# Global-filter mixing and a SoLU layer on one core: the opening's x from one queue, tables and weights requested during the first step

## The chip, the cores and the metric

The kernel runs on one core of one Trainium2 chip. The metric is the device time of one execution in microseconds (us). A core has TensorE (PE; its weight loads are listed as PEld), VectorE (DVE), ScalarE (ACT), GpSimd (POOL) and SyncE (SP). SP, ACT and POOL each have a queue on which they request DMA transfers; SP's and ACT's queues are of the hardware kind (q1 and q10 in the profile), POOL's is of the software kind (q0).

## The reference, cut to what matters

```python
# x: (8, 3136, 256); filt_r, filt_i: (1569, 256); float32
X = np.fft.rfft(x, axis=1)                       # along the sequence
Y = X * (filt_r + 1j * filt_i)[None]
x = np.fft.irfft(Y, n=3136, axis=1).reshape(25088, 256)

h = x @ w_in                                     # (25088, 1024), float64 weights in memory
e = np.exp(h - h.max(-1, keepdims=True))
solu = h * e / (e.sum(-1, keepdims=True) + 1e-9)
mu = solu.mean(-1, keepdims=True); var = ((solu - mu) ** 2).mean(-1, keepdims=True)
out = ((solu - mu) / np.sqrt(var + 1e-6) * g_ln) @ w_out   # (25088, 256)
```

## The kernel before

The transform of length 3136 = 49 x 64 is done in steps by matrix products: a first step over 49 rows (with tables `wf`), a second step over the 64 columns (tables `de`), the product with the filter, and the two steps back. Between the steps the data change their layout by going through DRAM (`d1`, `d2`). The first of the eight batch entries is transformed alone, in an opening; the other seven are transformed beside the token blocks of the SoLU layer, step by step, in the long body. The opening also fetches the filter (`f`) and the tables, and fetches and converts the weights from float64.

The opening, cut to what the change and the text below touch. Line numbers in the profile: L465 is the transfer in `fetch_x`, L217 and L219 the product and the copy in `first`, L172 and L173 the two transfers of `by_16`, L425 and L428 the transfers of `load_tables`, L369 those of the weights, L381 to L405 the conversion of a weight, L516 the small fetches of the second step's first unit (t<-x), L282 those of its other units (y<-d), L292 the products of the second step, L492 the idle products, L313 to L315 the product with the filter, L548 the stores to `f_dram`.

```python
def by_16(dmas, out, in_):                       # 100 rows: 96 on one queue, 4 on the other
    n = 45 if out.shape[0] == N1 else out.shape[0] // 16 * 16
    dmas[0](out=out[:n], in_=in_[:n])
    dmas[1](out=out[n:], in_=in_[n:])

# in class Spectrum
def first(self, i, halves, ps, evac, out=None):
    ...
    for j, u in enumerate(halves):
        nc.tensor.matmul(out=ps[0:NK, j], lhsT=wf_t, rhs=self.xs[i][0:NR, 2*u:2*u+2, :], ...)
    evac(out=t1..., in_=ps...)                   # ACT copies back over x

# the opening
def load_tables(i0, n, dma):                     # n of 13 units, from i0
    de = fpool.tile([P, n, 2, 2, NQ], FP32, ...)
    dma(out=de, in_=de_dram[i0:i0 + n]...)
    f = fpool.tile([P, n, 2, C], FP32, ...)
    for place, k, held, rows in all_filter_rows(i0, n):      # 8 transfers
        dma(out=f[place, 0:held, k, :], in_=rows)

def begin(j): raws[j] = load_words(weights[j][1], j)         # POOL requests a weight, 512 KB

rows_x = pools["r"].tile([P, NH, C], FP32, name="x_0", tag="r")
def fetch_x(h, n0, n, r0, rows, dma):            # h = 0: columns upwards; h = 1: downwards
    first, step = (n0, C) if h == 0 else (N2 - 1 - n0, -C)
    dma(out=rows_x[N1*h + r0:N1*h + r0 + rows, n0:n0 + n], in_=...)

nc.sync.dma_start(out=wf_t, in_=wf_dram)
pieces = NH // NCH                               # 8 pieces of 4 columns
fetch_x(0, 0, NCH, 0, N1 - 1, nc.sync.dma_start)
fetch_x(0, 0, NH, N1 - 1, 1, nc.sync.dma_start)
for i in range(pieces):
    if i:
        fetch_x(0, NCH * i, NCH, 0, N1 - 1, nc.sync.dma_start)
    fetch_x(1, NCH * i, NCH, 0, N1, nc.gpsimd.dma_start)
    if i in (4, 7):
        begin(i // 7)                            # weights 0 and 1
load_tables(0, 4, nc.gpsimd.dma_start)
load_tables(4, 4, nc.gpsimd.dma_start)
for i in range(pieces):                          # the first step
    sp.xs[i] = rows_x[:, NCH * i:NCH * i + NCH]
    sp.first(i, (0, 1), ..., nc.scalar.copy, sp.xs[i][0:NK])
    sp.store_first(i, 0, lambda out, in_: by_16((nc.scalar.dma_start, nc.sync.dma_start), out, in_))

idle_row(8, "idle")                              # products of tables[0] that keep TensorE busy
for j in range(2):
    convert(j)                                   # VectorE, ACT (L400) and POOL: weights 0 and 1

sp.t2s[0] = t2_0 = pools["t2"].tile([P, 4, C], FP32, ...)
for n in range(16):                              # t<-x, 32 KB each, in turns on SP and ACT
    (nc.sync, nc.scalar)[n % 2].dma_start(out=t2_0[NH*(n%4):NH*(n%4)+NH, n//4, :],
                                          in_=rows_x[n:n + 1])
for i in range(1, units):                        # y<-d, 512 KB each (the last 128 KB)
    sp.fetch(i, nc.sync.dma_start, spare_piece(i - 1))
    if i == 2:
        load_tables(8, NP - 8, nc.sync.dma_start)
for i in range(2):
    start(i)                                     # pb: forward product of unit i
for i in range(units):                           # 7 units
    if i + 2 < units:
        start(i + 2)
    sp.multiply(i, 0, nc.vector.tensor_tensor)   # VectorE
    sp.multiply(i, 1, nc.gpsimd.tensor_tensor)   # VectorE and POOL
    ...                                          # inverse product, store; begin(2) to begin(6)
...                                              # step back, weights 2 to 7, fetch of entry 1
for i0, n, rows in ((0, 4, P), (4, 4, P), (8, NP - 9, P), (NP - 1, 1, NQ)):
    f, at = filters[i0]
    nc.sync.dma_start(out=f_dram[i0:i0 + n]..., in_=f[0:rows, at:at + n]...)
```

Of the kernel before, what the change touches and what calls it, by code (L numbers as in the profile page):

```python
# [17 lines left out]
P = 128  # L18
# [5 lines left out]
N1, N2 = 49, 64  # L24
NH = N2 // 2
NS, NQ = (N1 + 1) // 2, 64
NP = (NS + 1) // 2
NR = 2 * N1
NK = 4 * NS
NCH = 4  # L30
# [62 lines left out]
def kernel(  # L93
# [10 lines left out]
    nc = tc.nc  # L104
# [52 lines left out]
    def all_filter_rows(i0, n):  # L157

        for k, filt in enumerate((filt_r, filt_i)):
            for u in range(2):  # L160
                for quarter in range(2):
                    held = min(n, (NS - u + 1) // 2 - i0)
                    yield (slice(NQ * u + 32 * quarter, NQ * u + 32 * quarter + 32), k, held,
                           filter_rows(filt, quarter, u, i0, held))
# [4 lines left out]
    def by_16(dmas, out, in_):  # L169
# [5 lines that stand above are left out]
    class Spectrum:  # L175
# [24 lines left out]
        def fetch_x(self, i, halves, out=None):  # L200
            if out is None:
                out = self.pools["r"].tile([P, NCH, C], FP32, name=f"x_{self.e}_{i}", tag="r")
            self.xs[i] = out
            xb = x[self.e]
            for h, first, step in ((0, NCH * i, C), (1, N2 - 1 - NCH * i, -C)):
                halves[h](out[N1 * h:N1 * h + N1],
                          bass.AP(tensor=xb.tensor, offset=xb.offset + first * C,
                                  ap=[[N2 * C, N1], [step, NCH], [1, C]]))
# [151 lines left out]
    with ExitStack() as st:  # L360
# [6 lines left out]
        def load_words(src, n):  # L367
            raw = wpool.tile([P, 512, 2], I32, name=f"raw_{n}", tag="raw")
            nc.gpsimd.dma_start(  # L369
                out=raw.rearrange("p (k d) w -> p k d w", d=src.shape[-2]) if len(src.shape) == 4 else raw,  # L370
                in_=src)
            return raw
# [45 lines left out]
        def fetch_second():  # L418
            for i in range(6):
                second.fetch_x(i, [lambda out, in_: nc.sync.dma_start(out=out, in_=in_)] * 2,  # L420
                               spare_piece(i))

        def load_tables(i0, n, dma):
            de = fpool.tile([P, n, 2, 2, NQ], FP32, name=f"de_{i0}", tag=f"de{i0}")
            dma(out=de, in_=de_dram[i0:i0 + n].rearrange("i p k u q -> p i (k u q)"))  # L425
            f = fpool.tile([P, n, 2, C], FP32, name=f"f_{i0}", tag=f"f{i0}")
            for place, k, held, rows in all_filter_rows(i0, n):
                dma(out=f[place, 0:held, k, :], in_=rows)  # L428
            for i in range(n):
                tables[i0 + i], filters[i0 + i] = (de, i), (f, i)  # L430
# [12 lines left out]
        def resident(held):  # L443
            def find(sp, u):
                i, pairs = sp.units[u]
                tile, at = held[i]
                return tile[:, at:at + pairs]
            return find

        sp = Spectrum(0, pools, resident(filters), resident(tables))  # L450
        raws = {}

        def begin(j):
            raws[j] = load_words(weights[j][1], j)
# [15 lines left out]
        nc.sync.dma_start(out=wf_t, in_=wf_dram)  # L470
        pieces = NH // NCH

        fetch_x(0, 0, NCH, 0, N1 - 1, nc.sync.dma_start)
        fetch_x(0, 0, NH, N1 - 1, 1, nc.sync.dma_start)
        for i in range(pieces):
            if i:
                fetch_x(0, NCH * i, NCH, 0, N1 - 1, nc.sync.dma_start)
            fetch_x(1, NCH * i, NCH, 0, N1, nc.gpsimd.dma_start)
            if i in (4, 7):
                begin(i // 7)  # L480
        load_tables(0, 4, nc.gpsimd.dma_start)
        load_tables(4, 4, nc.gpsimd.dma_start)
        for i in range(pieces):
            sp.xs[i] = rows_x[:, NCH * i:NCH * i + NCH]

            sp.first(i, (0, 1), ps_h.tile([P, 2, 512], FP32, name=f"pa_0_{i}", tag="h"),
                     nc.scalar.copy, sp.xs[i][0:NK])
            sp.store_first(i, 0, lambda out, in_: by_16((nc.scalar.dma_start, nc.sync.dma_start), out, in_))

        def idle(out):  # L490

# [23 lines left out]
        for n in range(16):  # L515
            (nc.sync, nc.scalar)[n % 2].dma_start(  # L516
                out=t2_0[NH * (n % 4):NH * (n % 4) + NH, n // 4, :], in_=rows_x[n:n + 1])
# [25 lines left out]
        for ch in range(pieces):  # L543
            fetch_back(0, ch, None, by_16)
        fetch_second()
        for i0, n, rows in ((0, 4, P), (4, 4, P), (8, NP - 9, P), (NP - 1, 1, NQ)):
            f, at = filters[i0]
            nc.sync.dma_start(  # L548
                out=f_dram[i0:i0 + n].rearrange("i u q k c -> (u q) i (k c)")[0:rows],
                in_=f[0:rows, at:at + n].rearrange("p i k c -> p i (k c)"))  # L550
# [283 lines left out]
    for e in range(1, B):  # L834
        first_at, spectrum_at, back_at = PLAN[e]
        sp = Spectrum(e, pools, load_filter, load_de)
        if e == 1:
            sp = second
# [178 lines left out]
```

## Time and profile before

| | |
|---|---|
| time, median of 3 runs | 1681.72 us (1679.47 to 1682.98) |
| span of the profiled execution | 1680.2 us |
| PE, PEld, DVE, ACT, POOL busy | 95%, 65%, 75%, 56%, 67% |
| first matmul of the opening starts | 9.34 us |
| last store of the first step requested by ACT | 28.49 us |
| first product of the second step (pb) starts | 45.28 us |
| fourth unit's rows requested, used | 53.51, 59.24 us |
| mean DMA rate, whole span; 0 to 130 us | 186; 264 GB/s |

The profile comes from one execution, taken by the hardware profiler. Engine rows give busy time and what ended the idle time before a group of instructions; a row `t<-x` names the tile written and the tile read. A row with ACTq, SPq or POOL and DMA_DIRECT2D is the request of a transfer, not the transfer itself; the transfer's landing is seen in who was released by it. The chain of waits is followed back from the last instruction to what released it at each step. PEclk is the granted TensorE clock, where 1.00 is full speed.

### The profile page before, as it was taken

The page shows a single profiled execution, that of the slowest core. Times are in us where ns is not written, and L with a number is a line of the kernel's source. Part 1 is how long each engine was busy: PE and PEld are TensorE (multiplying, and loading weights), DVE is VectorE, ACT ScalarE, POOL GpSimd, SP SyncE. Part 2 cuts the span into 40 slices and gives each one's busy share as a digit, 9 for nine tenths or more (in the row PEclk, how much of TensorE's full clock was granted, in tenths as well). Part 3 has the DMA queues.
Part 4 walks back from the last instruction along what each step waited for, and adds up shares of the span by engine and source line. Part 5 has one row for each costly group of instructions (what it writes and reads, how often), then busy time and mean ns, then how long its engine had stood idle before and what let it go on. Part 6 is the DMA issues. An engine that isn't in the chain of part 4 may idle for free.

```text
span 1680.2 us, 31072 instructions
## 1 busy us (share of the span) xinstructions
PE 1597.7 (95%) x10022; PEld 1094.7 (65%) x10022; DVE 1260.4 (75%) x2619; ACT 939.3 (56%) x1730; POOL 1120.8 (67%) x1268
## 2 busy tenths in 40 slices
PE   5798899999999999999999999999999999999996
PEld 1353356766766676667766676667776777777776
DVE  1676887788777877886878777887778767787773
ACT  2154455656655565566655656556565566655551
POOL 4444786577676766697577866687576766676674
PEclk8999999999999999999999999999999999999999
DMA  9886868786787668865786667766775444444443
GB/s 264 254 278 202 255 180 243 196 220 182 191 224 222 178 182 236 228 182 150 210 243 195 176 166 220 229 181 161 204 213 161 117 125 123 103 106 105 109 112 95
DMA packets 375957, 311.72 MB, mean 186 GB/s; under 512 B 61514, under 2 KB 341571, under 8 KB 375795
## 3 DMA queue, kind: packets, MB, share of 16 engines
q1 hardware_dynamic: 306260, 169.81, 38.5%
q0 software_dynamic: 32640, 101.65, 20.5%
q10 hardware_dynamic: 36896, 38.28, 8.2%
q8 instruction: 81, 1.33, 0.3%
q14 instruction: 80, 0.66, 0.1%
HBM read 124.83 MB, written 81.50 MB: 123 GB/s over the span
## 4 chain that ended last, share of the span: by engine, by line
PE 64%; DMA 17%; DVE 8%; POOL 3%; issue 3%; SPq 2%; ACT 1%; ACTq 0%; DVEq 0%; POOLq 0%
PE m L680 26%; PE o L792 25%; DMA solu_t<-turn 7%; PE py L353 5%; DMA x<-in_x_dram 2%; DMA t<-d 2%; PE pa L260 2%; PE pb L292 2%; PE pc L292 2%; SPq L750 2%; DVE h L728 2%; DVE turn L738 1%; DMA out_dram<-ot 1%; PE pa L217 1%; DVE diff L245 1%
## 5 line engine op out<-in xcount | busy, mean ns | idle before, releaser
L730 ACT ACTIVATE e<-h,nmu 128x1024 f32<-128x1024 f32 x196 | 225.3, 1149 | 360.3 <-DVE h L728 358.8
L792 PEld LDWEIGHTS o<-w_out_sb,solu_t 128*128 128x128 f32 x3136 | 380.3, 192 | 57.8 <-issue 40.7
L792 PE MATMUL o<-w_out_sb,solu_t 128*128 128x128 f32 x3136 | 400.5, 276 | 9.1 <-DVE rsum L723 6.3
L680 PE MATMUL m<-w_in_sb,s 128*128 128x512 f32 x784 | 401.8, 604 | 4.6 <-ACT h L690 2.5
L792 PEld LDWEIGHTS o<-w_out_sb,u 128*128 128x128 f32 x2352 | 305.2, 191 | 147.4 <-issue 113.8
L658 POOL TENSOR_TENSOR u<-solu_t 128x512 f32<-128x512 f32 x98 | 145.3, 1483 | 311.0 <-DMA solu_t<-turn 179.0
L680 PE MATMUL m<-w_in_sb,y 128*128 128x512 f32 x588 | 313.8, 617 | 15.9 <-DVE nmax L704 12.8
L792 PE MATMUL o<-w_out_sb,u 128*128 128x128 f32 x2352 | 312.3, 276 | 7.0 <-ACT ot L804 6.3
L728 DVE SCALAR_TENSOR_TENSOR h<-e,rsum,h 128x1024 f32<-128x1024 f32 x196 | 289.1, 1475 | 6.9
L811 DVE SCALAR_TENSOR_TENSOR ot<-o,rs_t,ot 128x128 f32<-128x128 f32 x294 | 102.5, 349 | 206.6 <-ACT ot L804 170.3
L690 ACT COPY h<-m 128x512 f32<-128x512 f32 x294 | 173.5, 590 | 130.8 <-PE m L680 116.2
L738 DVE STREAM_TRANSPOSE turn<-h 128x1024 f32<-128x1024 f32 x196 | 242.3, 1236 | 0.8
L712 ACT ACTIVATE e<-h,nmax 128x1024 f32<-128x1024 f32 x196 | 226.1, 1154 | 0.0
L658 POOL TENSOR_TENSOR u<-solu_t,u 128x512 f32<-128x512 f32 x98 | 142.7, 1456 | 87.2 <-PE o L792 83.3
L704 DVE CUSTOM_DVE_ANT_0 h<-m,h 128x512 f32<-128x512 f32 x196 | 133.2, 679 | 82.2 <-ACT h L690 59.3
L680 PEld LDWEIGHTS m<-w_in_sb,y 128*128 128x128 f32 x588 | 95.1, 192 | 124.5 <-DVE nmax L704 67.9
L356 ACT COPY y<-py 128x392 f32<-128x392 f32 x128 | 109.6, 856 | 105.4 <-PE py L353 103.8
L353 PEld LDWEIGHTS py<-wi_t,t 100*128 100x128 f32 x1024 | 132.3, 192 | 53.9 <-issue 40.4
L680 PEld LDWEIGHTS m<-w_in_sb,s 128*128 128x128 f32 x784 | 124.0, 191 | 65.9 <-issue 45.7
L658 POOL TENSOR_TENSOR solu_t<-solu_t,solu_t 128x512 f32<-128x512 f32 x98 | 150.8, 1538 | 7.7
L658 POOL TENSOR_TENSOR u<-u,solu_t 128x512 f32<-128x512 f32 x98 | 136.9, 1397 | 0.7
L353 PE MATMUL py<-wi_t,t 100*128 100x98 f32 x1024 | 131.6, 273 | 0.7 <-DMA t<-d 0.4
(108 smaller groups left out, 1978.3 us busy)
## 6 DMA issues: line engine op xcount, KB each, us to landing
solu_t<-turn SPq DMA_DIRECT2D x784, 128.0 KB
out_dram<-ot SPq DMA_DIRECT2D x196, 128.0 KB
t<-d POOLq DMA_DIRECT2D x56, 400.0 KB, 4.9
d<-x POOLq DMA_DIRECT2D x100, 200.0 KB, 5.3
f<-f_dram POOLq DMA_DIRECT2D x39, 512.0 KB, 6.9
d<-g POOLq DMA_DIRECT2D x39, 512.0 KB, 5.1
t<-d ACTq DMA_DIRECT2D x36, 512.0 KB
x<-in_x_dram SPq DMA_DIRECT2D x112, 98.0 KB
```

Of the source, the lines that this page charges most:

```text
L353: nc.tensor.matmul(out=psv[:, i:2 * NCH - i:2 * NCH - 1 - 2 * i, :], lhsT=t4s[e, ch][:, i, cb * P:cb * P + P], rhs=wi_t, start=True, stop= ...
L356: evac(out=y[:, cb, t0:t0 + S].rearrange("p (r m j) -> p m j r", m=N2 // NCH, j=NCH)[:, ch:last + 1 - ch:last - 2 * ch], in_=psv.rearrange ...
L658: nc.gpsimd.tensor_tensor(out=out, in0=in0, in1=in1, op=op)
L680: nc.tensor.matmul(out=ms[j, bank], lhsT=lhsT, rhs=w_in_sb[:, w, :], start=m in (1, 2, 7), stop=True, skip_group_check=True)
L690: nc.scalar.copy(out=h_half(k, i), in_=ms[j, 0])
L704: nc.vector.tensor_tensor_reduce(out=h_half(k, i), in0=ms[j, bank], in1=h_half(*kept), scale=1.0, scalar=sofar, op0=ALU.add, op1=ALU.min, ...
L712: nc.scalar.activation(out=e, in_=hs[k], func=AFT.Exp, bias=nmaxs.pop(k)[:, 1:2], scale=-1.0, accum_out=esum)
L728: nc.vector.scalar_tensor_tensor(out=solu, in0=e, scalar=rsum, in1=solu, op0=ALU.mult, op1=ALU.mult, accum_out=nmu)
L730: nc.scalar.activation(out=e, in_=solu, func=AFT.Square, bias=nmu, scale=-float(DFF), accum_out=variances[g][:, i:i + 1])
L738: nc.vector.transpose(out=turns[g][:, :, i, :], in_=solus.pop(k).rearrange("p (f j) -> p f j", j=32))
L792: nc.tensor.matmul(out=pos[p, bank], lhsT=lhs[:, f, :], rhs=w[:, f, :], start=f == 0 and m in (1, 2, 7), stop=True, skip_group_check=True)
L811: nc.vector.scalar_tensor_tensor(out=ot, in0=pos[p, bank], scalar=rs, in1=out_half(p, *kept)[0], op0=ALU.mult, op1=ALU.add)
```

## The change

All x of the opening is now requested by SP, piece by piece, both halves of a piece behind each other; the second half's 49 rows are cut into 45 for each piece and 4 rows once for all columns. POOL requests nothing until the first step's pieces are done: then it stores the last four rows of each piece (this was SP's), and asks for the tables of units 0 and 1 of 13 after the third piece, weight 0 after the fifth, tables 2 and 3 after the sixth, weight 1 after the eighth, and then tables 4 to 7. The purpose is that x, which the first step needs, does not share the DMA engines with what is needed later. The copy of the filter to `f_dram` follows the new cut of the tables.

```diff
-        fetch_x(0, 0, NCH, 0, N1 - 1, nc.sync.dma_start)
-        fetch_x(0, 0, NH, N1 - 1, 1, nc.sync.dma_start)
         for i in range(pieces):
-            if i:
-                fetch_x(0, NCH * i, NCH, 0, N1 - 1, nc.sync.dma_start)
-            fetch_x(1, NCH * i, NCH, 0, N1, nc.gpsimd.dma_start)
-            if i in (4, 7):
-                begin(i // 7)
-        load_tables(0, 4, nc.gpsimd.dma_start)
-        load_tables(4, 4, nc.gpsimd.dma_start)
+            for h in range(2):
+                rows = (N1 - 1, N1 - 4)[h]
+                fetch_x(h, NCH * i, NCH, 0, rows, nc.sync.dma_start)
+                if i == 0:
+                    fetch_x(h, 0, NH, rows, N1 - rows, nc.sync.dma_start)
         for i in range(pieces):
             sp.xs[i] = rows_x[:, NCH * i:NCH * i + NCH]
 
             sp.first(i, (0, 1), ps_h.tile([P, 2, 512], FP32, name=f"pa_0_{i}", tag="h"),
                      nc.scalar.copy, sp.xs[i][0:NK])
-            sp.store_first(i, 0, lambda out, in_: by_16((nc.scalar.dma_start, nc.sync.dma_start), out, in_))
+            sp.store_first(i, 0, lambda out, in_: by_16((nc.scalar.dma_start, nc.gpsimd.dma_start), out, in_))
+            if i in (2, 5):
+                load_tables(2 * (i // 5), 2, nc.gpsimd.dma_start)
+            elif i in (4, 7):
+                begin(i // 7)
+        load_tables(4, 4, nc.gpsimd.dma_start)
 ...
-        for i0, n, rows in ((0, 4, P), (4, 4, P), (8, NP - 9, P), (NP - 1, 1, NQ)):
+        for i0, n, rows in ((0, 2, P), (2, 2, P), (4, 4, P), (8, NP - 9, P), (NP - 1, 1, NQ)):
             f, at = filters[i0]
             nc.sync.dma_start(
```

## The prediction

> **What bounds the kernel now.** I read the page first, for the whole: TensorE is busy 95% of the span, and the chain of waits that ends last is 64% TensorE. So the body is set by TensorE. Then stage by stage, because the change lies wholly ahead of the body. The rows below are of the view of busy time by stage: start:end, length, then busy us and count for PE, PEld, DVE, ACT and POOL, then the granted clock, the DMA share and GB/s.
>
> ```profile
> 15.00:30.00 15.00, 11.42 (x26) 4.10 (x24) 7.06 (x16) 8.18 (x9) 5.11 (x9) 0.98 1.03 355
> 30.00:45.00 15.00, 8.96 (x16) 3.20 (x16) 0.47 (x1) 0.14 (x1) 10.61 (x14) 0.68 0.89 209
> 45.00:60.00 15.00, 7.76 (x75) 4.13 (x78) 9.54 (x15) 1.07 (x2) 6.34 (x7) 0.89 0.96 255
> 120.00:1680.00 1560.00, 1508.81 (x9584) 1049.84 (x9582) 1193.30 (x2496) 902.55 (x1681) 1065.19 (x1196) 0.99 0.66 180
> ```
>
> The reader is to see two kernels in one. After 120 us TensorE is busy 1508.81 of 1560 us and nothing in the diff touches it. Before 60 us the DMA engines are nearly full while the others idle, and in the stretch 30 to 45 us they are full (0.89) at only 209 GB/s, against 355 just before.
>
> Next the chain in order of time (start, us, what), the opening:
>
> ```profile
> 1.35 7.95 DMA x<-in_x_dram
> 9.34 8.51 PE pa L217 x12
> ...
> 26.70 6.53 DMA d<-x
> 33.25 8.10 DMA t<-x
> 41.37 4.71 DMA t<-x
> 46.09 7.40 DMA f<-in_filt_r_dram
> 53.51 5.59 DMA y<-d
> 59.24 2.01 PE pb L292 x16
> ```
>
> Up to 26 us it is the arrival of the first x piece and then TensorE's eight pieces; from 26.70 to 59.10 it is transfers alone: the last store of the first step, the sixteen small fetches of the second step's first unit (t<-x), the third part of the tables, then the fourth unit's rows. The timelines of the queues and of VectorE say why they follow each other:
>
> ```profile
> 28.90 1.24 ACT L400 ACTIVATE raw<-raw 128x512 f32<-128x512 int32 x2 [0.78 <-DVE power L388]
> 29.87 13.29 ACTq L516 DMA_DIRECT2D t<-x  x8
> ...
> 30.81 11.06 SPq L516 DMA_DIRECT2D t<-x  x8
> 42.05 1.50 SPq L282 DMA_DIRECT2D y<-d  x2
> ...
> 64.42 0.69 DVE L313 TENSOR_TENSOR pr<-pb,f 128x512 f32<-128x512 f32 x1 [6.41 <-PE pc L292]
> ```
>
> SP asks for y<-d only at 42.05, when its eight t<-x are out, and VectorE, having done three units of the product with the filter by 58.0, stands 6.41 us for the fourth. From there to 107 us VectorE is nearly always busy (49.91 of the 60 us from 60 to 120), so what the fourth unit loses is passed on.
>
> **What the Trainium skill says.** "DMA: Bandwidth & Descriptors", section Queues, rings and completion order: each DMA engine takes turns between the queues that have work for it, packet by packet. The trace agrees in kind: between 15 and 35 us, with stores on ACT's queue and tables, weights and late x on POOL's, the two moved 3.21 and 3.41 MB. The same page, section Why a DMA increments its semaphore by 16 and not by 1: an SP or ACT transfer uses the largest number of engines, up to 16, that divides its outer size. So 48 rows use 16, 45 rows 15, 49 rows only 7, 4 rows 4. That is what the cut into 45 and 4 rows is for; no view here shows single engines. "TensorE: Matmul & The Clock Gate", Part 1: the array runs at half clock until it has been busy for some 3.4 us. The trace agrees: the first pieces take 3.4 us each (12.87 minus 9.34 us, about), from 15.4 us on 1.72, and the clock falls to 0.52 between 30 and 40 us.
>
> **The change part by part.**
>
> 1. x on one queue. POOL's first x transfer was issued at 1.35 and landed at 9.30, beside SP's seven other pieces of the first half. Now the first piece (192 + 32 + 180 + 128 KB) is alone in front. 532 KB at the 190 GB/s of the first 15 us is 2.8 us; SP issues from 0.72 at about 0.45 us each, the first packets move at about 2, and the four-row transfer with 32 KB on each of four engines adds 1 to 2 us of tail. I put the piece at 7.0 instead of 9.3: 2.3 us won. TensorE sets the pace after that (two pieces at 3.4, six at 1.72), and x needs 400 KB per 1.72 us, 233 GB/s, with the engines almost to itself. The last copy, at 27.11 before, also loses a wait of 1.35 us that now has no reason: it starts at about 24.5 to 25.
>
> 2. Tables and weights later. POOL now starts them when the third piece has been copied, about 16.5 us. Up to the second weight it has 3 stores of the last four rows that wait for nothing new, 9 table transfers, 2 stores, weight 0, 1 store, 9 tables, 2 stores: 24 issues or so at 0.57 to 0.77 us, thus 15 to 17 us with some waits. Weight 1 is issued at about 32 to 34 and lands, at 4 to 6 us, at 37 to 40. Before it had landed at 26.5. This matters because ACT converts it (L400) in the row **ahead of** its eight t<-x: those went out from 29.87 and now cannot before about 38. That is a loss of 8 us for half of the first unit.
>
> 3. What SP does meanwhile. In the order of the built program SP now issues its eight t<-x, two y<-d, the third tables' de and five of its eight f transfers without needing anything from ACT; ACT's eight in turn reuse the semaphores of those y<-d, de and f, and so wait until they have landed. Before, the two queues went in turns and SP's y<-d stood behind ACT's. So 2.4 MB (2x512, 640, 3x160, 2x128 KB) move from behind t<-x to ahead of its second half. They can start at about 31 instead of 42. Against 1.57 MB of tables and 0.5 MB of weight still on POOL's queue, some 4.5 MB from 31 us at about 300 GB/s (between the 209 and the 355 of the rows above) is 15 us: 46. ACT's last t<-x then land at about 49, against 47.7 before.
>
> 4. Sum. The first unit's product starts on VectorE at about 50.5 instead of 48.36, of which 1 to 1.5 is half clock: the eight idle matmuls that warm TensorE wait for the smaller first table alone, so they run by about 34 and are over long before pb. Three units at 3.2 us bring 60.1. The fourth unit's rows are asked for right after ACT's fourth t<-x and are there by 52 to 55, so the 6.41 us stand goes nearly away, and the fourth unit starts at about 60.5 instead of 64.42: **4 us won**. Of the parts: 2.3 from x early and about 6 from the stand, less about 4 for the late second weight and the cold clock.
>
> 5. The fifth f_dram store adds one issue of about 0.3 us on SP near 108 us, where a chain of f_dram waits stands (5.83 us); up to 0.5 us lost. All else after 60 us is the same instructions in the same order. TensorE waits only 42 us in all after 120, so a shift passes through: 1681.7 - 4 + 0.3 = **1678.0**.
>
> **The rivals.** *The second weight becomes the wait.* If POOL's issues, each waiting for the landing of the eighth before it, take 1.3 us as in before (18 in the 23.3 us from 15.54 to 38.88), weight 1 lands at 45 to 48, ACT's t<-x at 54 to 56, VectorE starts at 56 and the fourth unit at 66: 2 us lost, 1684. For it: the median landing of those f was 6.8 to 10 us. Against: the transfers are half the size now, and x no longer shares the queue. *Everything is bandwidth.* The bytes before the fourth unit are the same, and the engines were 0.9 to 1.0 full; then only order changes and the time stays within 1 us. Against: 209 GB/s in 30 to 45 us shows that these full engines were moving little. *The gain is whole.* If weight 1 lands by 35, the first unit is ready at 44 to 45 and the fourth at 55: 9 us won, 1672.5.
>
> **Range and chances.** The middle case is 1678.0; the first rival gives 1684, the last 1672.5; three runs of before already spread by 3.5 us. I take 1671.5 to 1684.5. A 2% step is 33.6 us, more than half of the whole opening to 60 us, so either outer chance is 1%.
>
> **What would show it.** In the profile after: the first matmul near 7.0 instead of 9.34 (step 1); the raw conversion on ACT near 38 followed by its t<-x (step 2); SP's y<-d near 31, well before ACT's t<-x (step 3); VectorE's first filter product near 50.5 and no stand over 2 us before the fourth unit, which starts near 60.5 (step 4); all after 120 us shifted by the same 4 us. The prediction is wrong if POOL's issues stretch past 36 us for weight 1, if x alone on one queue moves slower than 233 GB/s so that TensorE waits between pieces, or if the body takes the shift back by other DMA waits.

## The result, and the profile after

The changed kernel takes **1695.03 us** (median of 4 runs, 1691.81 to 1698.69) against 1681.32 us for the kernel before (4 runs, 1679.47 to 1682.98): ratio **1.0082, 95% interval 1.0059 to 1.0106**, 13.7 us slower. It lies outside the predicted range, on the other side of the kernel before than predicted.

The profiled execution has a span of 1694.2 us (before 1680.2). Behind the edit the lines of the changed kernel are three higher than before: the t<-x stand at L519 for L516, the idle products at L495 for L492. The view of busy time by stage, columns as before:

```profile
0.00:15.00 15.00, 5.28 (x7) 1.94 (x8) 0.06 (x1) 2.29 (x2) 0.42 (x5) 1.00 0.70 178
15.00:30.00 15.00, 11.92 (x27) 4.35 (x25) 0.00 (x0) 7.08 (x7) 10.34 (x19) 1.00 0.88 274
30.00:45.00 15.00, 8.62 (x16) 3.60 (x16) 3.79 (x8) 0.70 (x1) 7.82 (x15) 0.84 0.89 247
45.00:60.00 15.00, 1.64 (x6) 0.57 (x6) 3.77 (x8) 0.68 (x1) 7.74 (x9) 0.50 0.93 238
```

The DMA share in 0 to 30 us fell from 0.88 and 1.03 to 0.70 and 0.88, and the rates from 190 and 355 GB/s to 178 and 274. Times 15 us each, 8.2 MB had moved by 30 us before and 6.8 MB now. From 45 to 60 us TensorE was busy for 1.64 us instead of 7.76.

The chain of waits, pieces of it in the opening (start, us, what):

```profile
1.69 4.83 DMA x<-in_x_dram
6.54 3.17 DMA x<-in_x_dram
9.72 17.22 PE pa L217 x32
30.32 8.61 DMA t<-x
40.88 15.49 DMA f<-in_filt_r_dram
56.40 0.51 ACTq L519
58.24 4.42 DMA t<-x
88.26 12.21 PE idler L495 x28
```

The first matmul starts at 9.72 (before 9.34). After TensorE's eight pieces the chain goes through a table transfer `f` of SP's (units 8 to 12), which holds no data of the first unit; at 56.40 its landing releases one of ACT's requests (ACTq L519), and so the chain comes back to `t<-x`. The last row is the idle products that TensorE runs ahead of the step back; they lie behind the whole second step, and their start is used below as the mark of how late the opening is: **88.2 us, before 78.8**. (The timeline has 88.19.)

The timelines of POOL, VectorE, ACT and SP say how that came about. POOL first:

```profile
27.39 0.57 POOL L369 DMA_DIRECT2D raw<-in_moe_w_in_dram  x1
...
37.31 1.67 POOL L428 DMA_DIRECT2D f<-in_filt_i_dram  x3 [4.66 <-DMA raw<-in_moe_w_in_dram]
...
40.02 0.56 POOL L369 DMA_DIRECT2D raw<-in_moe_w_in_dram  x1
```

VectorE, ACT and SP:

```profile
47.83 0.43 DVE L381 TENSOR_SCALAR raw<-raw 128x512 int32<-128x512 int32 x1 [6.82 <-DMA raw<-in_moe_w_in_dram]
48.29 0.68 ACT L400 ACTIVATE raw<-raw 128x512 f32<-128x512 int32 x1 [10.09 <-DVE raw L381]
48.30 10.54 ACTq L519 DMA_DIRECT2D t<-x  x8
37.57 1.16 SPq L282 DMA_DIRECT2D y<-d  x2
63.84 0.69 DVE L313 TENSOR_TENSOR pr<-pb,f 128x512 f32<-128x512 f32 x1 [12.08 <-PE pb L292]
...
73.42 0.67 DVE L313 TENSOR_TENSOR pr<-pb,f 128x512 f32<-128x512 f32 x1
```

Weight 1 was requested at 40.02 and had landed at 47.83 (before 26.54). ACT stood 10.09 us for it and only then began its eight t<-x, which took 10.54 us to issue. The first product with the filter on VectorE starts at 63.84 (before 48.36), the fourth at 73.42 (before 64.42). The stand ahead of the fourth unit is gone, as its row has no wait, but everything ahead of it came 15 us later.

After the opening, the first of the 196 token blocks (start of its transpose on VectorE, L741, before L738) is 10.7 us later than before, block 80 is 13.5 later, and the last 13.9.

### The profile page after: what moved, and what is told of

It is laid out like the page before. It is cut to its first block, busy times and chain, and to the rows that moved or that the text cites. A ratio compares the mean times of both kernels' runs of the same rounds, so it can differ in the third digit from the quotient of the medians.

```text
span 1694.2 us, 31084 instructions
## 1 busy us (share of the span) xinstructions
PE 1603.3 (95%) x10022; PEld 1099.7 (65%) x10022; DVE 1270.7 (75%) x2619; ACT 938.7 (55%) x1730; POOL 1125.7 (66%) x1277
## 4 chain that ended last, share of the span: by engine, by line
PE 63%; DMA 16%; DVE 9%; issue 3%; SPq 3%; POOL 3%; ACT 3%; ACTq 0%; DVEq 0%; POOLq 0%
PE m L683 25%; PE o L795 24%; DMA solu_t<-turn 6%; PE py L353 5%; DMA x<-in_x_dram 3%; DVE h L731 2%; DMA t<-d 2%; SPq L753 2%; PE pc L292 2%; PE pb L292 2%; PE pa L260 2%; PE pa L217 2%; DVE turn L741 1%; DMA out_dram<-ot 1%; DVE diff L245 1%
## 5 line engine op out<-in xcount | busy, mean ns | idle before, releaser
L795 PE MATMUL o<-w_out_sb,solu_t 128*128 128x128 f32 x3136 | 403.0, 277 | 10.1 <-DVE rsum L726 7.2
L731 DVE SCALAR_TENSOR_TENSOR h<-e,rsum,h 128x1024 f32<-128x1024 f32 x196 | 295.2, 1506 | 6.9
L741 DVE STREAM_TRANSPOSE turn<-h 128x1024 f32<-128x1024 f32 x196 | 242.2, 1236 | 0.8
L661 POOL TENSOR_TENSOR u<-u,solu_t 128x512 f32<-128x512 f32 x98 | 140.9, 1438 | 0.7
```

Of the source, the lines that this page charges most:

```text
L661: nc.gpsimd.tensor_tensor(out=out, in0=in0, in1=in1, op=op)
L731: nc.vector.scalar_tensor_tensor(out=solu, in0=e, scalar=rsum, in1=solu, op0=ALU.mult, op1=ALU.mult, accum_out=nmu)
L741: nc.vector.transpose(out=turns[g][:, :, i, :], in_=solus.pop(k).rearrange("p (f j) -> p f j", j=32))
L795: nc.tensor.matmul(out=pos[p, bank], lhsT=lhs[:, f, :], rhs=w[:, f, :], start=f == 0 and m in (1, 2, 7), stop=True, skip_group_check=True)
```

## The experiments

Two theories at the start. **Lateness:** with tables and weights requested only from 20 us on, the DMA engines have too little to do in the first 30 us, weight 1 comes late, and what isn't moved is missing later. **Order:** ACT's half of the first unit's t<-x stands behind the second weight's conversion, and reuses semaphores of SP's y<-d, de and f, so that it waits for transfers that it doesn't need. A third, the rival of the prediction, is that the x part alone does harm. Ratios are against the kernel before on the same chip, whose times there spread wider (1675.0 to 1696.2) than in the first comparison; the mark is the start of the idle row in one profile. That one execution is not always a typical one: the first profile of e2 shows the fastest of its 12 executions, that of e7 the fastest of its 20, that of e10 the slowest of its 22.

| kernel | ratio, 95% interval | mark, us | first, fourth filter product |
|---|---|---|---|
| before (first profile) | | 78.8 | 48.36, 64.42 |
| changed (first profile) | 1.0082 (1.0059 to 1.0106) | 88.2 | 63.84, 73.42 |
| changed, again | 1.0060 (1.0040 to 1.0079) | 86.9 | 62.55, 72.13 |
| e1 weights first | 1.0034 (1.0016 to 1.0052) | 84.1 | 54.22, 69.48 |
| e2 conversion behind t<-x | 1.0038 (1.0011 to 1.0064) | 83.2, again 86.7 | 50.57, 68.81 |
| e3 x part only | 1.0066 (1.0048 to 1.0084) | 88.5 | 58.17, 74.13 |
| e4 late part only | 1.0037 (1.0019 to 1.0054) | 87.2 | 63.19, 72.76 |
| e5 before, weights late | 1.0011 (0.9988 to 1.0033) | 80.6 | 56.64, 66.21 |
| e6 = e2 + unit 3 ahead | 1.0035 (1.0022 to 1.0049) | 85.3 | 51.50, 66.04 |
| e7 before, unit 3 ahead | 1.0000 (0.9982 to 1.0017) | 78.6 | 48.87, 58.45 |
| e8 = e6 + long rows cut | 1.0005 (0.9990 to 1.0021) | 83.0 | 56.20, 65.76 |
| e9 = e2 + earlier requests | 1.0020 (1.0000 to 1.0040) | 79.6, again 81.6 | 52.45, 65.17 |
| e10 = e2 + tables behind x | 1.0011 (0.9998 to 1.0025) | 88.5, again 87.9 | 56.10, 73.19 |
| e12 before, conversion behind | 1.0003 (0.9986 to 1.0019) | 77.4 | 48.55, 63.00 |
| e13 changed + earlier requests | 1.0051 (1.0035 to 1.0066) | 83.1 | 59.07, 68.63 |

### Each part alone: e3 and e4

e3 takes x from SP alone and keeps the early requests of tables and weights, which now go out at once, since POOL's own x no longer stands ahead of them (weight 0 had landed at 7.43 us there, at 19.48 before); e4 takes x from two queues as before and keeps the late requests.

```diff
 e3, against before
-            fetch_x(0, ...)   # SP          fetch_x(1, ...)   # POOL
-            if i in (4, 7): begin(i // 7)
+            for h in range(2): ...           # as in the change: both halves on SP
+        for j in range(2): begin(j)          # POOL, at once
 e4, against the changed kernel
-            for h in range(2): ...           # both halves on SP
+            fetch_x(0, ...)   # SP          fetch_x(1, ...)   # POOL
```

> The first part of the change alone: x from SP's queue with the cut 45 and 4 rows; POOL asks for both weights and then all tables at once as before, and the 4-row stores stay on SP. Theory A: within 4 us of the kernel before (1678 to 1686 us), as ACT finds both weights landed. Theory C (x on one queue is itself slow: the 4-row transfer on four engines, 1 KB packets, SP held by its own x): about as slow as the changed kernel, 1690 to 1697 us.

> The second part alone: x from two queues as before, tables and weights asked for during the first step as in the changed kernel. Theory A: the loss is all here, first filter product near 63 us, 1691 to 1698 us. Theory C: close to the kernel before, 1679 to 1686 us.

e3 was 0.66% slower; its TensorE and SP timelines:

```profile
18.21 5.52 PE L217 MATMUL pa<-x,wf_t 98*100 98x512 f32 x8 [18.21 <-DMA x<-in_x_dram]
...
1.19 32.58 SPq L465 DMA_DIRECT2D x<-in_x_dram  x18
```

The first matmul waits until 18.21 for x, and SP needs 32.58 us to issue eighteen transfers (14.03 in the changed kernel). Beside POOL's tables and weights, all requested from the start, x on a single queue is starved. So e3 does not show the x part by itself: it shows it against an earlier competition than before. "DMA: Bandwidth & Descriptors" of the Trainium skill, section Issuing engines are not separate DMA queues, says that transfers of all issuing engines end on the same 16 DMA engines and interleave there; this run agrees: SP's x had a queue to itself and still came at 18.21.

e4 has its mark at 87.2, between the two of the changed kernel (88.2 and 86.9), and like it had moved 6.8 MB by 30 us: the late requests carry the whole shift of the opening, as far as single profiles tell, and the x part brings nothing on top of them. Its ratio, 1.0037, is smaller than the changed kernel's all the same (1.0082 and 1.0060), for which see the section on the body.

### What is late: e1 and e5

e1 requests both weights on POOL ahead of everything in the changed kernel. e5 leaves the kernel before as it is and only requests its weights behind all tables.

```diff
 e1, against the changed kernel
+        begin(0)
+        begin(1)                             # ahead of x
-            elif i in (4, 7):
-                begin(i // 7)
 e5, against before
-            if i in (4, 7):
-                begin(i // 7)
         load_tables(4, 4, nc.gpsimd.dma_start)
+        for j in range(2):
+            begin(j)
```

> The changed kernel, but POOL asks for weights 0 and 1 before anything else; x from one queue and the late tables stay. Theory A (the second weight's late landing, 47.8 us, holds ACT's conversion and with it ACT's half of t<-x, and so the first unit): ACT's t<-x are issued from about 28.5 us, the first filter product on VectorE starts at 46 to 50 us instead of 63.8, the fourth unit at 57 to 65, time 1676 to 1684 us. Theory B (the tables themselves, late and small, and the transfers on SP's queue in 1 KB packets are the bound, whatever ACT waits for): first product not before 58 us, time 1689 to 1696 us.

> The kernel before, with one thing of the change: POOL asks for weights 0 and 1 behind all its tables instead of among the x. x from two queues, tables at once. The semaphores of ACT's t<-x are here those of SP's t<-x, hardly those of later transfers. Theory A (the second weight's landing in front of ACT's t<-x is enough for the loss): ACT's t<-x leave at the landing of weight 1, about 40 to 46 us, and eight of them take about 5 us, so the first filter product starts at 52 to 58 us instead of 48.4, the time is 3 to 8 us longer than before. Theory D (the loss in the changed kernel needs the crossed semaphores, which made ACT's t<-x wait for the last tables as well): first product within 2 us of before and time within 2 us.

e1 had ACT's t<-x out from 33.80 instead of 48.30, at the price of a first matmul at 12.97, and its mark at 84.1: 3 to 4 us of the 8 to 9 came back. The first product, at 54.22, lies between what the two theories had (50 at the latest, 58 at the earliest). e5, ACT and VectorE:

```profile
46.87 5.08 ACTq L516 DMA_DIRECT2D t<-x  x8
...
56.64 0.69 DVE L313 TENSOR_TENSOR pr<-pb,f 128x512 f32<-128x512 f32 x1 [4.24 <-PE pb L292]
...
66.21 0.68 DVE L313 TENSOR_TENSOR pr<-pb,f 128x512 f32<-128x512 f32 x1
```

Here weight 1 landed at 46.42, almost as late as in the changed kernel, and ACT's t<-x began at 46.87. The first product came 8.3 us later than before, yet the fourth only 1.8 later, because it takes over the 6.41 us stand. The ratio, 1.0011, has an interval that takes in 1. So a late second weight **by itself** costs far less than the change: in e5 the tables were early, the engines had moved 190 and 331 GB/s in the first two stretches (7.8 MB by 30 us), and ACT's eight t<-x took 5.08 us to issue instead of 10.54. Which of these differences counts, e5 alone doesn't tell.

### The order on ACT: e2, e12, e13

e2 moves the conversion of weights 0 and 1 behind the sixteen t<-x in the changed kernel; e12 does so in the kernel before; e13 leaves the conversion where it is and makes the requests earlier.

```diff
 e2 (and e12), against the changed kernel (and before)
-        for j in range(2):
-            convert(j)
         for n in range(16):                  # t<-x
             ...
+        for j in range(2):
+            convert(j)
 e13, against the changed kernel
-            if i in (2, 5):
-                load_tables(2 * (i // 5), 2, nc.gpsimd.dma_start)
-            elif i in (4, 7):
-                begin(i // 7)
+            if i in (0, 3):
+                load_tables(2 * (i // 3), 2, nc.gpsimd.dma_start)
+            elif i in (2, 5):
+                begin(i // 5)
```

> The changed kernel, but the conversion of weights 0 and 1 stands behind the sixteen t<-x in the program, so that the weights stay late and ACT's t<-x no longer stand behind them. Theory A: as with the weights first, ACT's t<-x from about 28.5 us, first filter product at 46 to 52 us, time 1676 to 1685 us. Theory B: first product not before 58 us, 1689 to 1696 us. If this one stays slow and the kernel with the weights first is fast, the weight hurts elsewhere (VectorE's conversion ahead of the filter product, POOL).

> The version with the conversion behind t<-x alone once more, one look: the idle row at 83.2 us within 1.5, if the opening repeats; then the 3.6 us of the earlier requests stand clear of the spread between executions.

> The kernel before, with the conversion of weights 0 and 1 moved behind the sixteen t<-x and nothing else. In the kernel before the second weight's conversion on ACT ended at about 29.9, 1.4 us after ACT's last store, so ACT's t<-x can begin 1.4 us earlier at most. Theory (bytes set the opening, and nothing stands behind a weight there): the idle row ahead of the step back within 1 us of 78.8, time the same within 1.5 us. Rival (a wait of ACT is worth its full length whatever the bytes): 1.4 us earlier or more, ratio 0.999 or less.

> The changed kernel with the tables of units 0 to 3 requested after pieces 0 and 3 and weights 0 and 1 after pieces 2 and 5, and the conversion left ahead of t<-x as in the changed kernel. If lateness is the whole cause (weight 1 lands at 41 instead of 47.8 us, so ACT's t<-x go out at 41.5): the idle row ahead of the step back at 82 to 84 us instead of 88.2, ratio 1.002 to 1.004. If the order of waits is a cause of its own (ACT's t<-x reuse the semaphores of SP's y<-d, de and f, and wait for their landing however early the weight comes): 86 us or later, ratio 1.005 or more.

e2, ACT and VectorE:

```profile
28.05 14.72 ACTq L516 DMA_DIRECT2D t<-x  x8
...
50.57 0.69 DVE L313 TENSOR_TENSOR pr<-pb,f 128x512 f32<-128x512 f32 x1 [0.21 <-PE pb L292]
...
60.31 0.69 DVE L313 TENSOR_TENSOR pr<-pb,f 128x512 f32<-128x512 f32 x1 [3.41 <-PE pc L292]
68.81 0.69 DVE L313 TENSOR_TENSOR pr<-pb,f 128x512 f32<-128x512 f32 x1 [5.29 <-PE pc L292]
```

The first product is back at 50.57 from 63.84, but stands of 3.41 and 5.29 us ahead of the third and fourth units appear, and the mark comes back to 83.2 in one profile and 86.7 in the other, whose first and fourth products are at 52.82 and 72.29. Of 13 us won at the first unit 0.2 to 5 reach the mark, depending on the profiles compared, and the time stayed 0.38% above before, where theory A had it at most 0.2% above. In the kernel before (e12) the same move brought 1.4 us at the mark and nothing in the time.

e13 is the test of the prediction's third step, as weight 1 landed at 38.65 there, inside the 37 to 40 that the prediction had assumed. The timelines of SP, VectorE and ACT; the last ACTq row is the second half of the row above it:

```profile
38.07 0.36 SPq L425 DMA_DIRECT2D de<-de_tbl  x1
38.65 0.43 DVE L381 TENSOR_SCALAR raw<-raw 128x512 int32<-128x512 int32 x1 [5.64 <-DMA raw<-in_moe_w_in_dram]
39.39 15.37 ACTq L518 DMA_DIRECT2D t<-x  x8
51.52 3.23 ACTq L518 DMA_DIRECT2D t<-x  x4
59.07 0.69 DVE L313 TENSOR_TENSOR pr<-pb,f 128x512 f32<-128x512 f32 x1 [16.18 <-PE pb L292]
```

ACT began its eight t<-x at 39.39 and was done issuing only at 54.76. The trace records by number which semaphore each request waits for and when a transfer raises it. ACT's fourth request was out by 42.01; the fifth waited for the semaphore of SP's `de`, asked for at 38.07 and landed at 51.50, and went out at 51.52. The sixth waited for one of SP's `f`, landed at 52.94, and went out at 52.96. The fifth t<-x landed at 55.96, and pb, which had begun on the rows that were there, went on at 56.01. (The profile's chain names y<-d and two `f` at this place; the semaphores show that the products waited for t<-x, and t<-x for `de` and `f`.) With the weight in time the first product still starts at 59.07. That is the crossing of semaphores, and in the changed kernel the same records show it: there `de` landed at 52.67 and held ACT's third request until 52.69, and two of `f`, landed at 54.25 and 56.38, held the fourth and the fifth until 54.27 and 56.40.

In e5 and e2 no t<-x of ACT's waits for SP's `de` or `f`. (In e2 the eight also take 14.72 us, since stores and SP's t<-x have to land first, but they begin 11 us earlier and end at 42.77.) So moving the conversion behind t<-x takes away the stand and the crossing together, and e5 has the stand without the crossing. "DMA: Bandwidth & Descriptors" of the Trainium skill, section Why a DMA increments its semaphore by 16 and not by 1, tells what a shared semaphore risks: with two transfers in flight on it, a wait can pass before the first has fully landed. In this case's traces the second request is held back until the first has landed, as above.

The mark of e13 is 83.1, 4 to 5 us better than the changed kernel, as expected if lateness were the whole cause; its ratio, 1.0051, is what was expected if the order of waits were a cause of its own. The run did not decide between the two.

### Dose and order of the requests: e9, e10

e9 is e2 with the earlier requests of e13. e10 is e2 with the tables of units 0 to 7 on SP directly behind x, and the weights on POOL after pieces 2 and 5.

```diff
 e10, against e2
+        load_tables(0, 2, nc.sync.dma_start)
+        load_tables(2, 2, nc.sync.dma_start)
+        load_tables(4, 4, nc.sync.dma_start)
-            if i in (2, 5):
-                load_tables(2 * (i // 5), 2, nc.gpsimd.dma_start)
-            elif i in (4, 7):
-                begin(i // 7)
-        load_tables(4, 4, nc.gpsimd.dma_start)
+            if i in (2, 5):
+                begin(i // 5)
```

> The version with the conversion of the weights moved behind t<-x, and beside it the tables of units 0 to 3 requested after pieces 0 and 3 (instead of 2 and 5), weights 0 and 1 after pieces 2 and 5 (instead of 4 and 7). Theory (the DMA engines have too little to do in the first 30 us, and the bytes not moved there are missing to the end of the second step): MB moved by 30 us rises by 0.5 to 0.9 from 6.92, and the idle row that stands ahead of the step back starts at 80.5 to 82 us instead of 83.2; the time falls by about 2 us against the version without the earlier requests. Rival (the order of waits on ACT and SP is what is left, not the bytes): the idle row stays within 1 us of 83.2.

> The version with the conversion behind t<-x and earlier requests once more, one look: the idle row at 79.6 us within 1.5, if the opening repeats from execution to execution.

> The version with the conversion moved behind t<-x, and the tables of units 0 to 7 requested by SP directly behind the last x, in the same queue, so that x stays first and the queue doesn't run empty; weights on POOL after pieces 2 and 5. Theory (underfilled engines): MB by 30 us at 7.5 to 8.1 (before 8.05), the idle row ahead of the step back at 79 to 81 us, although SP's t<-x now stand behind 27 requests of tables and start at 33 to 38 instead of 27.7. Rival (the order of waits is what counts): SP's later t<-x move pb of the first unit from 50 to 55 or later and the idle row goes to 85 or later although the bytes are there.

> The version with the tables behind x on SP once more, one look. If its first profile stood for all its executions: the idle row ahead of the step back at 88.5 us within 1.5. If that execution's opening was an unusually late one: 84 us or earlier.

e9, VectorE:

```profile
52.45 0.69 DVE L313 TENSOR_TENSOR pr<-pb,f 128x512 f32<-128x512 f32 x1 [7.46 <-PE pb L292]
...
65.17 0.69 DVE L313 TENSOR_TENSOR pr<-pb,f 128x512 f32<-128x512 f32 x1 [3.07 <-PE pc L292]
```

Its marks are 79.6 and 81.6. With the means of two profiles where there are two, the mark goes from 87.5 (changed) to 83.1 by earlier requests alone and from 85.0 (e2) to 80.6 by the same step with the conversion behind: 4.4 us both times. The conversion behind t<-x brings 87.5 to 85.0 and 83.1 to 80.6: 2.5 us both times. That these agree so well is in part luck: two profiles of one kernel differ by 1.3, 2.0 and 3.5 us, and the repeats of e9 and e2 both fell outside the 1.5 us that was expected. What is left to before's 78.8 is 1.8 us.

The times rank the two the other way. Earlier requests brought the ratio from 1.0060 to 1.0051 and from 1.0038 to 1.0020, 1.5 and 3 us; the conversion behind t<-x from 1.0060 to 1.0038 and from 1.0051 to 1.0020, some 4 and 5 us. With intervals of about 0.2% on each side no one of these steps is clear of noise. What the times do show is both together: e9, at 1.0020, took back two thirds of the changed kernel's 1.0060, with intervals that just touch.

The bytes explain what the earlier requests bring only in part. By 30 us e9 had moved 7.3 MB against 6.9 in e2, less than the 0.5 MB expected at least. By 60 us the mean rates over the whole stretch, 242 GB/s in e9 (250 again) and 237 in e2 (229 again), make a difference of 0.8 MB in the mean, some 3 us at the 270 GB/s that the kernel before moves from 60 to 90 us. That the bytes are the cause isn't shown: a later unit also requests its data later, and e8 below, with 6.8 MB by 30 us no more than the changed kernel, has its mark at 83.0.

e10, SP:

```profile
16.19 13.37 SPq L428 DMA_DIRECT2D f<-in_filt_r_dram  x4
...
46.61 5.07 SPq L516 DMA_DIRECT2D t<-x  x8
```

SP took 13.37 us to issue four of its 27 transfers of tables, and its own t<-x could only follow at 46.61 instead of 27.70. The rate between 15 and 30 us was 293 GB/s (e2: 286), so the queue behind x didn't fill the engines either: the theory's expectation fell, and the rival's (85 or later) came. Requests wait in line on SP like work on any engine.

### Where the stand goes: e6, e7, e8

e7 is the kernel before with the fourth unit's rows requested ahead of the third tables; e6 is e2 with the same edit; e8 is e6 with the one-row and four-row transfers of x cut into the first piece's four columns and the rest, the rest requested behind the first piece.

```diff
 e6, e7
-            if i == 2:
+            if i == 3:
                 load_tables(8, NP - 8, nc.sync.dma_start)
 e8, further
-                    fetch_x(h, 0, NH, rows, N1 - rows, nc.sync.dma_start)
+                    fetch_x(h, 0, NCH, rows, N1 - rows, nc.sync.dma_start)
+            if i == 0:
+                for h in range(2):
+                    rows = (N1 - 1, N1 - 4)[h]
+                    fetch_x(h, NCH, NH - NCH, rows, N1 - rows, nc.sync.dma_start)
```

> The kernel before with unit 3's rows asked for ahead of the tables 8 to 12. The fourth unit stood 6.4 us on VectorE. If its place in SP's row was the cause: fourth unit at 58 to 60 us instead of 64.4, the fifth at 62 to 66 instead of 67.6, time 2 to 5 us less than before. If bandwidth is the cause: the stand moves to the fifth unit and the time is within 1.5 us of before.

> The changed kernel with the conversion behind the t<-x (as in the second run) and with the rows of unit 3 asked for ahead of the tables 8 to 12 on SP. What was left of the loss in the second run was the fourth unit's stand (68.8 us against 64.4 before), which I put down to its rows standing behind those tables in SP's row. If so, the fourth unit starts at 60 to 63 us, the fifth may now stand for the tables, the idle products of the middle start at 78 to 81 us (83.2 in the second run, 78.8 before) and the time is 1 to 5 us shorter than in the second run. If the stand is plain bandwidth (all bytes late), the fifth unit starts no earlier than in the second run (71.9 us) and the time is the same.

> The changed kernel with the conversion behind the t<-x, unit 3's rows ahead of the last tables, and the first piece freed from the long transfers: the four rows and the one row are asked for the first piece's four columns, and for the other columns behind it. If the 4-row transfer on few engines held the first piece (it landed at 9.8 us, while the 45 rows had landed at 7.7), the first matmul starts at 5.5 to 7.5 us instead of 9.7; the second piece then stands for the long transfers until about 10. With the rest as in the run beside it, the idle products of the middle start 1 to 3 us earlier than there and the time is 1675 to 1681 us where before is 1681.

e7, VectorE:

```profile
58.45 0.68 DVE L313 TENSOR_TENSOR pr<-pb,f 128x512 f32<-128x512 f32 x1
67.39 0.69 DVE L313 TENSOR_TENSOR pr<-pb,f 128x512 f32<-128x512 f32 x1 [5.70 <-PE pc L292]
```

The fourth unit came 6 us earlier, and the stand, now 5.70 us, moved to the fifth. Mark and time stayed (78.6, ratio 1.0000). In the kernel before, the stand that the prediction wanted to save is thus worth nothing by itself: another order puts it elsewhere, as was expected if bandwidth is the cause. In e6 it likewise only moved: VectorE stands 3.63 us ahead of the third unit and 3.64 ahead of the sixth, and neither mark nor time is clearly better than e2's, against what was expected.

e8, TensorE:

```profile
5.17 3.70 PE L217 MATMUL pa<-x,wf_t 98*100 98x512 f32 x4 [5.17 <-DMA x<-in_x_dram]
10.46 13.82 PE L217 MATMUL pa<-x,wf_t 98*100 98x512 f32 x24 [1.58 <-DMA x<-in_x_dram]
28.27 3.70 PE L217 MATMUL pa<-x,wf_t 98*100 98x512 f32 x4 [4.00 <-DMA x<-in_x_dram]
```

The first matmul starts at 5.17 instead of 9.72: the long rows had held the first piece. But now the rest of those rows comes too late, TensorE waits 1.58 and then 4.00 us, and the first step ends later than in the changed kernel. The mark, 83.0, is 2.3 us better than e6's, which two profiles of one kernel can also differ by; but in time e8 is 5 us faster than e6 on the same chip (1.0005 and 1.0035, with intervals that just fail to meet). It comes closest to the kernel before of all that request x from SP alone; expected were 1675 to 1681 us where before is 1681. So once the first piece is freed of the long rows, most of the loss in time is gone; no run tries this without the other two edits.

### The body: e11, and what stays open

> The changed kernel once more, on the chip of these runs. If the opening's shift is all there is, the difference to the kernel before is 9.4 us (ratio 1.0056); if the body adds its 4.6 us as in the first profile, 14 us (1.0083). The idle row ahead of the step back at 88 us within 1 in either case.

The changed kernel, run once more, gave ratio 1.0060 and a mark of 86.9. In its profile and in the first one, the shift against before's profile at the first token block was 9.6 and 10.7 us, at block 40 it was 16.4 and 16.6, at the end 14.2 and 13.9. But the body drifts by several us between executions of one kernel: the two profiles of e2 had shifts of 5.7 and 7.5 at the first block and 2.4 and 8.7 at the last; those of e10 10.1 and 8.3, then 12.2 and 2.8. e7's profile ran off the other way, from -0.3 to -4.9. So a single profile tells the opening to 1 to 3 us and the whole time only to about 6.

That is why the two columns of the table don't always go together. Three kernels have a late mark and took little time: e4 (87.2; interval 3.2 to 9.1 us at 1685.6) and, clearest, e10 (88.5 and 87.9; interval -0.3 to 4.2 us), and less so e8. In e10 some 5 to 10 us of the opening's shift must be made up in the body in most executions; e13 goes the other way, with 8.6 us in time for 4.3 at the mark. No profile shows a place: between blocks 40 and 80 the shift of e10's second profile falls by 4.6 us, but it falls by 2.4 to 4.4 in all others but e9's first, so that fall belongs to the profile of the kernel before. Why the body makes up or adds time stays open. No version beat the kernel before.

## Why the prediction was wrong, point by point

**Step 1, x on one queue: failed, by the tail of the four-row transfer.** The step put that tail at 1 to 2 us and the first matmul at 7.0; it was 9.72, 0.4 later than before. By the semaphores in the trace, the first piece's 45 rows had landed by about 4.8 on all but one DMA engine (7.5 there), which is where the step's 2.8 us from about 2 put them, and the four-row transfer on its four engines at 6.8, 7.5, 8.0 and 9.6. So the tail is about 4.7 us, and the whole 2.3 us of gain was lost to it; e8 shows the 5.17 that lie beneath. The rest of the step held: TensorE ran its eight pieces through in 17.20 us without a wait. The last copy started at 26.96, instead of 24.5 to 25, which is the same miss.

**Step 2, the second weight: right in kind, three terms too small.** POOL's issues did stretch past 36 us, the sign of being wrong that the prediction named: weight 1 was requested at 40.02. They began at 20.18 instead of 16.5, of which 2.7 us is step 1's miss. From there to the request of weight 1 were 19.8 us instead of 15 to 17; 4.66 of them POOL stood for weight 0, which took 9.7 us to land. Weight 1 then took 7.8 us instead of 4 to 6. Together the landing came at 47.83 instead of 37 to 40. The first rival had 45 to 48 from the landings of the kernel before, and was right on it.

**Step 3, SP's part: the order and the crossing right, the landings too early.** SP did ask for its y<-d ahead of ACT's t<-x, at 37.57 (not 31: its own eight t<-x took 9.53 us to issue). The step saw that ACT's eight reuse the semaphores of y<-d, de and f, put the landing of those at 46 and that of ACT's last t<-x at 49. e13 has the assumed weight; there `de` landed at 51.50 and the next two `f` at 52.94 and 53.34, the last request went out at 54.15 to 54.76, and the first product came at 59.07 instead of 50.5. By that run some 8.6 of the 13.3 us of this miss are in this step, 4.8 in step 2 (e13 also has its tables earlier, so the split is rough). The estimate of 15 us for the bytes took a rate of 300 GB/s from 31 us on; from 30 to 45 and from 45 to 60 us 267 and 210 were moved in e13, 247 and 238 in the changed kernel.

**Step 4, the sum: the stand went as said, the gain did not follow.** There is no stand ahead of the fourth unit. But the step counted the stand as time to be won, and e7 shows that in the kernel before it is not. The cold TensorE came as the step had it: the idle products were over by 38.9 (34 was said), and the clock is 0.50 from 45 to 60 us, where pb begins at 55.88. (The prediction saw the 3.4 us of the skill confirmed in its trace. By its own figures the slow rate lasted from 9.34 to about 15.4 us, some 6 us of work; 3.4 us is what one piece takes at that rate.) The fourth unit started at 73.42 instead of 60.5.

**Under all four: what the late requests leave undone.** The prediction read DMA engines 0.9 to 1.0 full and took the bytes as given, only put in another order. The change left 1.4 MB unmoved in the first 30 us. No step priced that; e4 shows the late requests alone to bring the whole shift at the mark, and e9 and e13 show requests two pieces earlier to be worth some 4 us of it. That the bytes themselves are the cause, and not the order of the waits, is not shown. The rival that everything is bandwidth named the quantity and drew the wrong conclusion, that time would stay within 1 us.

**Step 5 and the passing on.** The fifth f_dram store was not tried by itself. The shift did pass through the body, 9.4 us at the mark and 13.9 at the end, with a drift between executions of the size of the difference.

The first rival was the nearest, 1684 against 1695, and it too fell short, since it let the fourth unit slip by 2 us only, where it slipped by 9. Its numbers came true in e5, which has a late weight and no crossing: the first product at 56.64 and the fourth at 66.21, where it had said 56 and 66.

## What to carry to other kernels

When early transfers are held back to clear the way for one, count the bytes that the stretch no longer moves, and where they are to be moved instead: here 1.4 of 8.2 MB were put off, and no version of the change got the whole opening back. Ahead of an engine that only issues transfers, look for work in its row (a conversion that waits for a weight) and for semaphores that it shares with another queue, since both make it wait for data that it doesn't need; a stand that one order removes counts as a gain only once a run with just that order has shown it. A transfer of few long rows can hold a whole piece: cut it to what the first piece needs, and see that the rest still comes in time.

## What the runs showed of the hardware

- One row of x, 32 KB in one piece, moved as a single packet of 32,768 bytes in 2.19 us on one DMA engine; the four rows of the other half went in packets of 1 KB on four engines, and the slowest landed 4.7 us after most of the 45 rows requested just before them.
- From 2 to 18 us, SP's packets of 1 KB (x of the second half) in the changed kernel took 67 ns each in the mean, POOL's packets of 4 KB before 266 ns: by the byte the same.
- Eight requests of t<-x on ACT took 5.08 us in e5 and 15.37 in e13. In e5 they follow each other every 0.64 us; in e13 10 us of the 15.37 are one wait, that of the fifth request for the landing of `de`.
